# A fused attention and expert kernel: low halves of x written at once, all keys in one buffer, expert weights started a chunk earlier

## The chip, the cores and the metric

The kernel runs on one core of a Trainium2 chip. A core has a matrix engine (PE, whose weight loads are listed apart as PEld), a vector engine (DVE), a scalar engine (ACT), a GpSimd engine (POOL) and a queue engine (SP) that here only starts transfers. Each works through its own instructions in order, and they wait for one another through semaphores. The metric is device time in microseconds (us), the median of several runs.

## What is computed

Attention over 2 batches, 12 heads, 448 positions and head size 64, with a mix over heads ahead of the softmax and another behind it; then two expert layers on the 896 tokens.

```python
scores = scale * np.matmul(q, k.transpose(0, 1, 3, 2))
scores = np.einsum('bhij,hg->bgij', scores, w_pre)
attn = np.exp(scores - max); attn = attn / (sum + 1e-09)
attn = np.einsum('bhij,hg->bgij', attn, w_post)
x = np.matmul(attn, v)                 # -> [896, 768]
h = x @ w_in;  g = h * clip(h + 3, 0, 6) / 6;  x = g @ w_out
h = x @ w2_in; g = P(h) / Q(|h|);               out = g @ w2_out
```

Expert weights arrive as 64-bit numbers and are converted on the chip. Matrix products that must be exact are made of three: each operand is split into a high part (rounded to fp32r) and a low part (the rest), and high·high, high·low and low·high are added.

## The kernel before

**Attention.** Each batch has four chunks of query rows (12, 12, 12 and 9 groups of ten rows), eight chunks in all, numbered 0 to 7. The loop at L541 goes over chunks, the loop at L564 over the groups of a chunk. One pass of it is called a step here, and "step 6.11" is group 11 of chunk 6. There are 90 steps. The order of instructions on every engine is the order in which this code is written (a manual schedule).

In a step PE does, in this order: M, the head mix of this group's scores (`premix`, L277 to L279); A, the head mix of the weights of two groups ago (`postmix`, L312, eight entries); X, the product with the values (`av_unit`, L332, 16 matmuls) in some steps, for the chunk before; and scores of the next chunk (sc, L246) in some steps. DVE takes the maximum of M (L281), ACT the exponential e (L283). In the next step ACT copies A out (at, L316) and scales the mixing weights by the reciprocal sums (wr, L296). PE's A for a group waits for its wr. POOL splits the scores of the group two steps ahead into sh and sl (`gsplit`, L265, L267).

Two lists delay work: `preps` are run on ACT right behind the exponential of the next step, and their VectorE half (`lows`) a step later; `xposts` are run on ACT ahead of the next step's exponential and on DVE behind its maximum.

**Keys and x.** `XH` and `XL` hold the high and low part of x for the experts. While attention runs they lend their room: the keys of batch 0 (high and low) lie in XH, those of batch 1 in XL (L181). Batch 1's keys are loaded and split two at a time in chunks 0, 1 and 2 (L554). So x of the first 688 tokens goes to a separate `x1` when X leaves PSUM (L346 to L349), and is split into XH and XL later: `x_hi` copies 568 columns per row block in steps 6.0 to 6.5 (L614), `x_split` the remaining 120 columns and the whole low part, 688 columns, in steps 7.0 to 7.5 (L612). Later tokens are split straight out of PSUM (L351 to L356).

**Experts' first weights.** At the start of chunk 7 the pool `front` (queries, keys, staging) is released and the pool `late` is opened in its room (L559). Two weight units (768 KB each) are loaded from ACT's queue; the table `WST` says how many passes of their conversion (`split_pieces`, L406 to L422) run in each step: ACT scale, DVE shift, two DVE merges, then POOL split. The first expert product (h) starts in step 7.7.

**Values.** `load_v` loads values by pairs of heads into three buffers (`vraw`), each when the X that used the buffer is done. For chunk 7 these loads come at the end of attention, behind step 7.8, where six X units run one after another (L637).

Of the kernel before, what the change touches and what calls it, by code (L numbers as in the profile page):

```python
# [24 lines left out]
NCH = 4  # L25
# [24 lines left out]
def fused_kernel(  # L50
# [56 lines left out]
    x1 = x1p.tile([128, KD, XRAW], F32, name="x1")  # L107
# [17 lines left out]
    def load_v(C, hp):  # L125
        if C < len(chunks):
            t = att.tile([JP, 2, JC * D], F32, tag="vraw", bufs=3, name=f"vraw{C}_{hp}")
            nc.sync.dma_start(out=t, in_=v[chunks[C][0], hp])
            vraw[(C, hp)] = t

# [50 lines left out]
    ksts = [x.rearrange("p c t -> p (c t)").rearrange("p (x h s) -> p x h s", x=2, s=S) for x in (XH, XL)]  # L181
# [27 lines left out]
    def k_prep(b, hp):  # L209
        src = kraw[(b, hp // 2)][:, hp % 2, :]  # L210
        hi, lo = ksts[b][:, 0, hp, :], ksts[b][:, 1, hp, :]
# [21 lines left out]
    def scores(C, hp, tags=("sc", "sc"), st=None):  # L233
        n = chunks[C][3] * GR
        kh, kl = ksts[chunks[C][0]][:, 0, hp, :], ksts[chunks[C][0]][:, 1, hp, :]
# [104 lines left out]
    def av_evac(C, h, X):  # L340
# [5 lines left out]
        if t0 < XRAW:  # L346
            take = [lambda: None, lambda: None]
            take[h != 7] = lambda: (nc.vector.tensor_copy if h != 7 else nc.scalar.copy)(out=x1[:, cs, ts_], in_=src)
            xposts.append(take)  # L349
        else:  # L350
            xposts.append([  # L351
                lambda: nc.scalar.activation(out=XH[:, cs, ts_], in_=src, func=AF.Copy),
                lambda: nc.vector.tensor_tensor(
                    out=XL[:, cs, ts_], in0=src, in1=XH[:, cs, ts_].bitcast(F32), op=ALU.subtract
                ),
            ])  # L356
# [117 lines left out]
    def x_hi(c, a, b):  # L474
        nc.scalar.activation(out=XH[:, c, a:b], in_=x1[:, c, a:b], func=AF.Copy)

    def x_split(c):
        xposts.append([
            lambda: x_hi(c, XEAR, XRAW),
            lambda: nc.vector.tensor_tensor(  # L480
                out=XL[:, c, :XRAW], in0=x1[:, c, :], in1=XH[:, c, :XRAW].bitcast(F32), op=ALU.subtract
            ),
        ])
# [53 lines left out]
    WST = [0, 0, 1, 2, 1, 1, 2, 1, 1]  # L537
# [3 lines left out]
    for C, (b, r0, n, G) in enumerate(chunks):  # L541
# [11 lines left out]
        if C < 3:  # L553
            add([lambda: load_k(1, C), lambda: k_prep(1, 2 * C), lambda: k_prep(1, 2 * C + 1)], [8, 10, 11])  # L554
# [3 lines left out]
        if nxt is None:  # L558
            front.release()  # L559
            pools["late"] = tc.alloc_tile_pool(name="late", bufs=1, side="right", reuse_waits="tile")  # L560
            load_unit(units[0], nc.scalar)
# [318 lines left out]
```

## Time and profile before

| | |
|---|---|
| median of 3 runs | 763.8 us (762.0 to 770.0) |
| profiled execution | 766.65 us, span 764.9 us |
| PE busy | 722.0 us (94%) |
| DVE, ACT, POOL busy | 540.3, 426.4, 256.7 us |
| mean granted PE clock | 0.984 |
| PE, idle in all for ACT's wr | 14.9 us |

The span is the time from the first to the last instruction of the profiled execution; the run's own time is 1.75 us longer. PE is busy for most of the span, so what matters is where PE is not busy or slow, and what it waits for there.

### The profile page before, as it was taken

The numbers are of one execution on the slowest core, as the hardware profiler recorded it, in microseconds if no ns is written. First come the engines' busy times: TensorE is split into PE (matmuls) and PEld (weight loads), VectorE is DVE, ScalarE is ACT, GpSimd is POOL, SyncE is SP. The second block draws the span as 40 slices with busy tenths as digits, with TensorE's granted clock in tenths as the row PEclk, the third lists the DMA queues.
The fourth block names the chain that finished last, engine by engine and source line by source line (L and its number), as shares of the span: only waits on it lengthen the run. The fifth ranks groups of instructions, "written<-read, shape, count | busy, mean of one in ns | idle before, by whom it ended". The sixth has DMA issues, their size and how long they took to land.

```text
span 764.9 us, 12178 instructions
## 1 busy us (share of the span) xinstructions
PE 722.0 (94%) x4457; PEld 620.7 (81%) x4457; DVE 540.3 (71%) x947; ACT 426.4 (56%) x862; POOL 256.7 (34%) x255
## 2 busy tenths in 40 slices
PE   5899999999997889999999999999999998999996
PEld 2567777777776879888888888889899887999986
DVE  5564655545447749767655555569999999999996
ACT  4586666667676534443431111247667566689872
POOL 1776665666667525444344444300000000000000
PEclk8899999999999999999999999999999999999999
DMA  6545445445334435343333333334433353401002
GB/s 188 179 133 166 123 130 183 138 136 149 111 115 142 133 100 155 112 124 97 98 110 106 103 97 100 122 109 137 124 124 124 124 165 125 134 31 63 1 1 83
DMA packets 63283, 89.76 MB, mean 117 GB/s; under 512 B 5172, under 2 KB 53880, under 8 KB 63224
## 3 DMA queue, kind: packets, MB, share of 16 engines
q1 hardware_dynamic: 61024, 86.98, 36.7%
q10 hardware_dynamic: 2136, 2.01, 0.9%
q8 instruction: 35, 0.57, 0.3%
q14 instruction: 24, 0.20, 0.1%
q0 software_dynamic: 64, 0.01, 0.1%
HBM read 66.87 MB, written 2.75 MB: 91 GB/s over the span
## 4 chain that ended last, share of the span: by engine, by line
PE 70%; DVE 17%; ACT 6%; DMA 4%; issue 2%; SPq 0%; ACTq 0%; DVEq 0%
PE h L362 8%; PE h L364 8%; PE h L363 8%; PE A L312 8%; PE X L332 5%; PE y L364 5%; PE y L363 5%; PE y L362 5%; PE sc L246 5%; PE M L277 4%; PE M L279 2%; PE M L278 2%; DVE st L281 2%; PE acc L363 2%; PE acc L364 2%
## 5 line engine op out<-in xcount | busy, mean ns | idle before, releaser
L362 PE MATMUL h<-xh,wh 128*128 128x512 f32 (+1 forms) x384 | 143.2, 373 | 2.9 <-DVE u L714 1.7
L364 PE MATMUL h<-xh,wl 128*128 128x512 f32 (+1 forms) x384 | 141.4, 369 | 2.1 <-DVE wl L425 2.1
L363 PE MATMUL h<-xl,wh 128*128 128x512 f32 (+1 forms) x384 | 141.8, 369 | 0.0
L406 ACT ACTIVATE wf<-wraw 128x768 f32<-128x768 f32 (+1 forms) x50 | 43.8, 876 | 124.0 <-POOL wl L422 102.8
L312 PEld LDWEIGHTS A<-wr,e 120*112 120x112 f32 x720 | 82.4, 177 | 32.6 <-ACT wr L296 29.3
L312 PE MATMUL A<-wr,e 120*112 120x120 f32 x720 | 92.2, 271 | 15.2 <-ACT wr L296 14.9
L267 POOL TENSOR_TENSOR sl<-full,sh 120x448 fp32r<-120x448 f32 x89 | 103.3, 1161 | 7.4
L281 DVE TENSOR_REDUCE st<-M 120x1 f32<-120x448 f32 x90 | 56.1, 623 | 70.1 <-PE M L279 65.7
L283 ACT ACTIVATE e<-M,st 120x448 f32<-120x448 f32 x90 | 57.1, 635 | 73.8 <-DVE st L281 73.6
L362 PEld LDWEIGHTS h<-xh,wh 128*128 128x128 f32 x384 | 72.8, 190 | 12.9 <-DVE u L714 2.8
L364 PEld LDWEIGHTS h<-xh,wl 128*128 128x128 f32 x384 | 73.0, 190 | 12.1 <-DVE wl L425 3.3
L265 POOL TENSOR_SCALAR sh<-full 120x448 fp32r<-120x448 f32 x89 | 53.1, 597 | 85.4 <-PE M L278 54.5
L408 DVE TENSOR_SCALAR wf<-wf 128x768 int32<-128x768 int32 (+1 forms) x50 | 27.4, 549 | 76.7 <-ACT wf L406 76.7
L363 PEld LDWEIGHTS h<-xl,wh 128*128 128x128 f32 x384 | 72.9, 190 | 8.0
L421 POOL TENSOR_SCALAR wh<-wf 128x768 fp32r<-128x768 f32 (+1 forms) x34 | 33.1, 975 | 137.5 <-PE h L363 57.1
L364 PE MATMUL y<-gh,wl 128*128 128x384 f32 x192 | 70.8, 368 | 0.0
L363 PE MATMUL y<-gl,wh 128*128 128x384 f32 x192 | 70.2, 366 | 0.0
L362 PE MATMUL y<-gh,wh 128*128 128x384 f32 x192 | 69.9, 364 | 0.0
L422 POOL TENSOR_TENSOR wl<-wf,wh 128x768 fp32r<-128x768 f32 (+1 forms) x34 | 65.8, 1934 | 2.8
L316 ACT ACTIVATE at<-A 112x480 f32<-112x480 f32 x90 | 51.6, 574 | 5.4 <-PE A L312 5.3
L414 DVE SCALAR_TENSOR_TENSOR wf<-wraw,icst,wf 128x768 int32<-128x768 int32 (+1 forms) x50 | 51.2, 1026 | 0.8
L410 DVE SCALAR_TENSOR_TENSOR wf<-wraw,icst,wf 128x768 int32<-128x768 int32 (+1 forms) x50 | 50.3, 1007 | 0.9
(118 smaller groups left out, 1523.3 us busy)
## 6 DMA issues: line engine op xcount, KB each, us to landing
wraw<-in_moe_w_in_dram SPq DMA_DIRECT2D x30, 768.0 KB
wraw<-in_moe_w_out_dram SPq DMA_DIRECT2D x28, 768.0 KB
full<-stg SPq DMA_DIRECT2D x60, 210.0 KB
vraw<-in_v_dram SPq DMA_DIRECT2D x48, 224.0 KB
full<-stg SPq DMA_DIRECT2D x24, 157.5 KB
wraw<-in_moe_w_out_dram SPq DMA_DIRECT2D x6, 512.0 KB
kraw<-in_k_dram SPq DMA_DIRECT2D x6, 448.0 KB
qraw<-in_q_dram SPq DMA_DIRECT2D x6, 360.0 KB
```

Of the source, the lines that this page charges most:

```text
L265: eng.tensor_scalar(out=sh[:r], in0=s[:r], scalar1=1.0, scalar2=0.0, op0=ALU.mult, op1=ALU.add)
L267: return eng.tensor_tensor(out=sl[:r], in0=s[:r], in1=sh[:r].bitcast(F32), op=ALU.subtract)
L281: nc.vector.tensor_reduce(out=st[:r, 0:1], in_=mt[:r, :S], op=ALU.max, axis=AX.X, negate=True)
L283: nc.scalar.activation(out=e[:r], in_=mt[:r, :S], func=AF.Exp, bias=st[:r, 0:1], accum_out=st[:r, 1:2])
L312: nc.tensor.matmul(av[:, jc], lhsT=e[:r, jc * JP : (jc + 1) * JP], rhs=wr[:r, :, :rr], start=True, stop=True)
L316: lambda: nc.scalar.activation(out=at[C][:, :, :, c0 : c0 + rr], in_=av, func=AF.Copy)
L362: nc.tensor.matmul(o, lhsT=wh, rhs=mh, start=first, stop=False)
L363: nc.tensor.matmul(o, lhsT=wh, rhs=ml, start=False, stop=False)
L364: nc.tensor.matmul(o, lhsT=wl, rhs=mh, start=False, stop=last)
L410: nc.vector.scalar_tensor_tensor(out=wi, in0=hw, scalar=icst[:, 0:1], in1=wi, op0=ALU.bitwise_and, op1=ALU.bitwise_or)
L414: nc.vector.scalar_tensor_tensor(out=wi, in0=lw, scalar=icst[:, 1:2], in1=wi, op0=ALU.logical_shift_right, op1=ALU.bitwise_or)
L422: nc.gpsimd.tensor_tensor(out=lv, in0=w, in1=hv.bitcast(F32), op=ALU.subtract)
```

## The change

Both batches' keys now share XH, so XL is free from the start. Batch 1's keys are loaded in steps 2.4 to 2.6 and split in steps 2.9 to 3.1 (ACT), after the last scores of batch 0. Every X is split as it leaves PSUM: ACT writes the high part to x1 (now of the rounded type) or XH, DVE writes the low part to XL. `x_split` and `x_hi` go; `x_move` copies the high parts from x1 to XH on ACT (568 columns, six times, in steps 6.10 to 7.3, and 6 x 120 columns in step 7.4). The pool `late` is opened at the end of step 6.8; its first two units are loaded from SP's queue; one conversion pass runs in every step from 6.11 on. The values of chunk 7 are loaded in step 7.1 by six transfers into a buffer of the tag `full`.

```diff
@@ -104,7 +104,7 @@
     XH = xp.tile([128, KD, NT], F32R, name="xh")
     XL = xp.tile([128, KD, NT], F32R, name="xl")
     XRAW = S + 2 * CH
-    x1 = x1p.tile([128, KD, XRAW], F32, name="x1")
+    x1 = x1p.tile([128, KD, XRAW], F32R, name="x1")
 
 
     qraw = {}
@@ -123,10 +123,18 @@
         kraw[(b, m)] = t
 
     def load_v(C, hp):
-        if C < len(chunks):
+        if C < len(chunks) - 1:
             t = att.tile([JP, 2, JC * D], F32, tag="vraw", bufs=3, name=f"vraw{C}_{hp}")
             nc.sync.dma_start(out=t, in_=v[chunks[C][0], hp])
             vraw[(C, hp)] = t
+
+    def load_vs():
+
+        C = len(chunks) - 1
+        t = att.tile([JP, NP, 2, JC * D], F32, tag="full", bufs=2, name="vlast")
+        for hp in range(NP):
+            nc.sync.dma_start(out=t[:, hp], in_=v[chunks[C][0], hp])
+            vraw[(C, hp)] = t[:, hp]
 
 
     BF16 = mybir.dt.bfloat16
@@ -178,7 +186,7 @@
 
 
 
-    ksts = [x.rearrange("p c t -> p (c t)").rearrange("p (x h s) -> p x h s", x=2, s=S) for x in (XH, XL)]
+    kst = XH.rearrange("p c t -> p (c t)").rearrange("p (x h s) -> p x h s", x=2, s=S)
     qr = front.tile([128, NP, CH], F32R, name="qr")
     ql = front.tile([128, NP, CH], F32R, name="ql")
 
@@ -208,7 +216,7 @@
 
     def k_prep(b, hp):
         src = kraw[(b, hp // 2)][:, hp % 2, :]
-        hi, lo = ksts[b][:, 0, hp, :], ksts[b][:, 1, hp, :]
+        hi, lo = kst[:, 0, hp, :], kst[:, 1, hp, :]
         preps.append([
             lambda: nc.scalar.activation(out=hi, in_=src, func=AF.Copy),
             lambda: nc.vector.tensor_tensor(out=lo, in0=src, in1=hi.bitcast(F32), op=ALU.subtract),
@@ -232,7 +240,7 @@
 
     def scores(C, hp, tags=("sc", "sc"), st=None):
         n = chunks[C][3] * GR
-        kh, kl = ksts[chunks[C][0]][:, 0, hp, :], ksts[chunks[C][0]][:, 1, hp, :]
+        kh, kl = kst[:, 0, hp, :], kst[:, 1, hp, :]
         if hp == 0:
             full[C] = att.tile([GP, MG, S], F32, tag="full", bufs=2, name=f"full{C}")
         room(2)
@@ -343,17 +351,11 @@
         t0 = b * S + r0
         src = X[:, :, :n]
         cs, ts_ = slice(c0, c0 + 2), slice(t0, t0 + n)
-        if t0 < XRAW:
-            take = [lambda: None, lambda: None]
-            take[h != 7] = lambda: (nc.vector.tensor_copy if h != 7 else nc.scalar.copy)(out=x1[:, cs, ts_], in_=src)
-            xposts.append(take)
-        else:
-            xposts.append([
-                lambda: nc.scalar.activation(out=XH[:, cs, ts_], in_=src, func=AF.Copy),
-                lambda: nc.vector.tensor_tensor(
-                    out=XL[:, cs, ts_], in0=src, in1=XH[:, cs, ts_].bitcast(F32), op=ALU.subtract
-                ),
-            ])
+        o = (x1 if t0 < XRAW else XH)[:, cs, ts_]
+        xposts.append([
+            lambda: nc.scalar.activation(out=o, in_=src, func=AF.Copy),
+            lambda: nc.vector.tensor_tensor(out=XL[:, cs, ts_], in0=src, in1=o.bitcast(F32), op=ALU.subtract),
+        ])
 
 
     pools = {}
@@ -471,16 +473,8 @@
     build_mix()
     XEAR = S + CH
 
-    def x_hi(c, a, b):
-        nc.scalar.activation(out=XH[:, c, a:b], in_=x1[:, c, a:b], func=AF.Copy)
-
-    def x_split(c):
-        xposts.append([
-            lambda: x_hi(c, XEAR, XRAW),
-            lambda: nc.vector.tensor_tensor(
-                out=XL[:, c, :XRAW], in0=x1[:, c, :], in1=XH[:, c, :XRAW].bitcast(F32), op=ALU.subtract
-            ),
-        ])
+    def x_move(cs, a, b):
+        preps.append([lambda: nc.scalar.copy(out=XH[:, cs, a:b], in_=x1[:, cs, a:b].bitcast(F32)), lambda: None])
 
     first = gsplit(0, nc.vector)
     gsplit(1)
@@ -534,7 +528,7 @@
     SST = {12: [0, 1, 3, 4, 6, 7], 9: [0, 1, 2, 3, 4, 5]}
     QST = {12: [8, 9], 9: [6, 7]}
     AVST = {12: [2, 5, 8, 9, 11, 11], 9: [2, 3, 5, 6, 8, 8]}
-    WST = [0, 0, 1, 2, 1, 1, 2, 1, 1]
+    PRE, LATE = B * NCH - 2, 9
     manual = tc.manual_schedule()
     manual.__enter__()
     m = 0
@@ -550,17 +544,14 @@
             add([lambda h=h: scores(nxt, h) for h in range(NP)], SST[G])
         if C + 2 < len(chunks):
             add([lambda: q_prep(C + 2, 0, NP // 2), lambda: q_prep(C + 2, NP // 2, NP)], QST[G])
-        if C < 3:
-            add([lambda: load_k(1, C), lambda: k_prep(1, 2 * C), lambda: k_prep(1, 2 * C + 1)], [8, 10, 11])
+        if C == NCH - 2:
+            add([lambda m=m: load_k(1, m) for m in range(3)], [4, 5, 6])
+            add([lambda h=h: k_prep(1, h) for h in range(NP - 1)], [8, 8, 9, 10, 11])
+        if C == NCH - 1:
+            add([lambda: k_prep(1, NP - 1)], [0])
         if C > 0:
             add([lambda h=h: av_unit(C - 1, h) for h in range(1, H, 2)], [("av", a) for a in AVST[G]])
 
-        if nxt is None:
-            front.release()
-            pools["late"] = tc.alloc_tile_pool(name="late", bufs=1, side="right", reuse_waits="tile")
-            load_unit(units[0], nc.scalar)
-            load_unit(units[1], nc.scalar)
-            ucur[0] = 2
         for s in range(G):
             if s == 0 and C + 2 < len(chunks):
                 load_q(C + 2)
@@ -588,30 +579,35 @@
             xposts.clear()
             posts.clear()
             banks_of.clear()
-            if nxt is None:
-                for _ in range(WST[s]):
-                    next(wpieces)
+            if C > PRE or (C == PRE and s == G - 1):
+                next(wpieces)
             if m >= LAG:
                 postmix(m - LAG)
             for u in sched.get(("av", s), []):
                 u()
             for u in sched.get(s, []):
                 u()
-            if nxt is None and s == 0:
+            if C == PRE and s == LATE - 1:
+                flush()
+                front.release()
+                pools["late"] = tc.alloc_tile_pool(name="late", bufs=1, side="right", reuse_waits="tile")
+                load_units(1)
                 wpieces = (p for u in units[:4] for p in split_pieces(u))
-            if nxt is None and s == 4:
+            if C == PRE and s >= LATE:
+                x_move(s - LATE, 0, XEAR)
+            if C > PRE and s < KD - 3:
+                x_move(s + 3, 0, XEAR)
+            if C > PRE and s == 3:
+                x_move(slice(0, KD), XEAR, XRAW)
+            if C > PRE and s == 1:
+                load_vs()
+            if C > PRE and s == 4:
                 load_units(2)
-            if nxt is None and s == 7:
-                load_units(3)
             if nxt is None and s >= 7:
                 if s == 7:
                     h100 = gemm1(0, 0, ps.tile([128, 512], F32, tag="sc", bufs=3, name="h1_0_0"))
                 for _ in range(3):
                     next(h100)
-            if nxt is None and s < KD:
-                x_split(s)
-            if nxt == len(chunks) - 1 and s < KD:
-                x_hi(s, 0, XEAR)
             m += 1
 
     C = len(chunks) - 1
@@ -633,7 +629,8 @@
     for _ in range(2):
         next(h110)
     drain()
-    pieces(3)
+    load_units(3)
+    pieces(2)
     for h in range(1, H, 2):
         av_unit(C, h)
         flush()
```

Where rows move. On ACT, in steps 6.11 to 7.1 (e is the exponential, at and wr belong to the two groups before, x is x1, xh is XH, wf is a weight unit); before:

```order
L283 ACTIVATE e_3000,st_2998<-M_2994,st_2998 120x448
L389 DMA wraw<-in_moe_w_in_dram 128x6x256 x2
L316 ACTIVATE at_2705<-A_3004 112x48x10
L296 ACTIVATE wr_3039<-wq,st_2976 120x120
L283 ACTIVATE e_3051,st_3049<-M_3045,st_3049 120x448
L316 ACTIVATE at_2705<-A_3056 112x48x10
L296 ACTIVATE wr_3062<-wq,st_2998 120x120
L475 ACTIVATE xh<-x_86 128x120
L283 ACTIVATE e_3075,st_3073<-M_3069,st_3073 120x448
```

and after the change:

```order
L291 ACTIVATE e_3020,st_3018<-M_3014,st_3018 120x448
L477 CAST xh<-x_86 128x568
L408 ACTIVATE wf<-wraw 128x768
L324 ACTIVATE at_2718<-A_3027 112x48x10
L304 ACTIVATE wr_3054<-wq,st_2994 120x120
L356 ACTIVATE x_86<-X_9_3032 128x2x120
L291 ACTIVATE e_3067,st_3065<-M_3061,st_3065 120x448
L477 CAST xh<-x_86 128x568
L324 ACTIVATE at_2718<-A_3074 112x48x10
L304 ACTIVATE wr_3080<-wq,st_3018 120x120
```

The two transfers have left this queue, and copies of x and a scaling pass stand between an exponential and the at and wr behind it.

On DVE, from the maximum of step 7.3 on; before:

```order
L281 TENSOR_REDUCE st_3135<-M_3131 120x1
L291 TENSOR_SCALAR st_3097<-st_3097 120x1
L292 RECIPROCAL st_3097<-st_3097 120x1
L480 TENSOR_TENSOR xl<-x_86,xh 128x688
L408 TENSOR_SCALAR wf<-wf 128x768
L410 SCALAR_TENSOR_TENSOR wf<-wraw,icst,wf 128x768
L281 TENSOR_REDUCE st_3172<-M_3168 120x1
L291 TENSOR_SCALAR st_3135<-st_3135 120x1
L292 RECIPROCAL st_3135<-st_3135 120x1
L353 TENSOR_TENSOR xl<-X_1_3112,xh 128x2x120
L480 TENSOR_TENSOR xl<-x_86,xh 128x688
L414 SCALAR_TENSOR_TENSOR wf<-wraw,icst,wf 128x768
```

and after the change:

```order
L289 TENSOR_REDUCE st_3157<-M_3153 120x1
L299 TENSOR_SCALAR st_3121<-st_3121 120x1
L300 RECIPROCAL st_3121<-st_3121 120x1
L289 TENSOR_REDUCE st_3197<-M_3193 120x1
L299 TENSOR_SCALAR st_3157<-st_3157 120x1
L300 RECIPROCAL st_3157<-st_3157 120x1
L357 TENSOR_TENSOR xl<-X_1_3135,xh 128x2x120
L410 TENSOR_SCALAR wf<-wf 128x768
L289 TENSOR_REDUCE st_3224<-M_3220 120x1
L299 TENSOR_SCALAR st_3197<-st_3197 120x1
L300 RECIPROCAL st_3197<-st_3197 120x1
L412 SCALAR_TENSOR_TENSOR wf<-wraw,icst,wf 128x768
```

The low parts of x of 688 columns are gone, and one weight pass at most stands between two maxima.

On SP's queue, from chunk 6's end on (vraw are values of chunks 6 and, second time round, 7; wraw weight units); before:

```order
L128 DMA vraw_5_2930<-in_v_dram 112x512
L128 DMA vraw_0_2962<-in_v_dram 112x512
L128 DMA vraw_1_3018<-in_v_dram 112x512
L128 DMA vraw_2_3028<-in_v_dram 112x512
L128 DMA vraw_3_3121<-in_v_dram 112x512
L128 DMA vraw_4_3157<-in_v_dram 112x512
L389 DMA wraw<-in_moe_w_in_dram 128x6x256
L128 DMA vraw_5_3227<-in_v_dram 112x512
L128 DMA vraw_0_3263<-in_v_dram 112x512
L389 DMA wraw<-in_moe_w_in_dram 128x6x256
L128 DMA vraw_1_3331<-in_v_dram 112x512
L128 DMA vraw_2_3341<-in_v_dram 112x512
```

and after the change:

```order
L128 DMA vraw_5_2940<-in_v_dram 112x512
L391 DMA wraw<-in_moe_w_in_dram 128x6x256 x2
L128 DMA vraw_0_2980<-in_v_dram 112x512
L128 DMA vraw_1_3041<-in_v_dram 112x512
L128 DMA vraw_2_3051<-in_v_dram 112x512
L136 DMA vlast<-in_v_dram 112x512 x6
L128 DMA vraw_3_3144<-in_v_dram 112x512
L128 DMA vraw_4_3183<-in_v_dram 112x512
L391 DMA wraw<-in_moe_w_in_dram 128x6x256
L128 DMA vraw_5_3245<-in_v_dram 112x512
L391 DMA wraw<-in_moe_w_in_dram 128x6x256 x13
```

Two weight units now stand ahead of chunk 6's values, and chunk 7's values ahead of the second half of those of chunk 6.

## Rows read from the trace of the kernel before

**Rows 1.** Waits of PE: engine, line, releaser, us in total, times, longest.
```profile
PE A L312 <- ACT wr L296: 14.9, 22, 2.0
PE X L332 <- DMA vraw<-in_v_dram: 2.8, 2, 1.5
```
**Rows 2.** Timeline of PE, steps 6.10 to 7.0: start, length, instruction [idle before].
```profile
227.38 1.04 PE L332 MATMUL X<-at,vraw 112*64 112x120 f32 x16
228.35 0.47 PE L277 MATMUL M<-sh,wp_h 120*120 120x448 f32 x1
...
229.07 0.98 PE L312 MATMUL A<-wr,e 120*112 120x120 f32 x8
229.81 0.44 PE L277 MATMUL M<-sh,wp_h 120*120 120x448 f32 x1
...
231.45 1.07 PE L312 MATMUL A<-wr,e 120*112 120x120 f32 x8 [0.78 <-ACT wr L296]
...
234.24 0.46 PE L277 MATMUL M<-sh,wp_h 120*120 120x448 f32 x1
```
**Rows 3.** Timeline of ACT in step 6.10.
```profile
229.93 0.64 ACT L283 ACTIVATE e<-M,st 120x448 f32<-120x448 f32 x1 [0.88 <-DVE st L281]
```
**Rows 4.** Timeline of PE, steps 7.5 to 7.8.
```profile
245.62 0.44 PE L277 MATMUL M<-sh,wp_h 120*120 120x448 f32 x1
...
248.39 1.07 PE L312 MATMUL A<-wr,e 120*112 120x120 f32 x8 [1.92 <-ACT wr L296]
...
250.37 0.46 PE L277 MATMUL M<-sh,wp_h 120*120 120x448 f32 x1
...
256.13 0.73 PE L277 MATMUL M<-sh,wp_h 120*120 120x448 f32 x1
...
259.86 0.36 PE L277 MATMUL M<-sh,wp_h 120*120 120x448 f32 x1
```
**Rows 5.** Timeline of DVE in the same stretch.
```profile
247.32 1.23 DVE L480 TENSOR_TENSOR xl<-x,xh 128x688 fp32r<-128x688 f32 x1
248.47 1.89 DVE L414 SCALAR_TENSOR_TENSOR wf<-wraw,icst,wf 128x768 int32<-128x768 int32 x1
250.28 0.61 DVE L281 TENSOR_REDUCE st<-M 120x1 f32<-120x448 f32 x1
```
**Rows 6.** The chain of work that ended last, three places: start, us, what.
```profile
204.05 0.57 ACT xh L475
...
251.65 0.79 ACT wf L406
...
268.26 2.00 PE X L332 x48
270.27 4.30 DMA vraw<-in_v_dram
274.62 1.44 PE X L332 x16
276.06 0.62 PE h L362
```
**Rows 7.** Stretches: us, PE, PEld, DVE, ACT, POOL busy, PE clock, DMA share, GB/s.
```profile
170.50:193.00 22.50, 22.50 (x186) 17.65 (x184) 11.94 (x35) 15.37 (x41) 15.42 (x19) 1.00 0.52 151
201.80:225.80 24.00, 23.23 (x186) 17.05 (x184) 11.97 (x35) 18.66 (x47) 15.34 (x18) 1.00 0.36 108
276.00:278.50 2.50, 2.50 (x11) 2.50 (x10) 0.90 (x2) 2.40 (x5) 0.00 (x0) 0.61 0.01 2
```
**Rows 8.** Groups by line and shape: count | busy us, mean ns | idle before.
```profile
L213 ACT ACTIVATE xl<-kraw 128x448 fp32r<-128x448 f32 x6 | 3.4, 568 | 0.0
L214 DVE TENSOR_TENSOR xl<-kraw,xl 128x448 fp32r<-128x448 f32 x6 | 6.4, 1072 | 0.0
L214 DVE TENSOR_TENSOR xh<-kraw,xh 128x448 fp32r<-128x448 f32 x6 | 3.6, 621 | 0.8 <-ACT xh L213 0.8
L352 ACT ACTIVATE xh<-X 128x240 fp32r<-128x240 f32 x3 | 1.1, 376 | 0.9 <-PE X L332 0.9
L353 DVE TENSOR_TENSOR xl<-X,xh 128x240 fp32r<-128x240 f32 x3 | 1.2, 395 | 1.5 <-ACT xh L352 1.5
```

## The prediction

> **What bounds the kernel now.** I read the page first: PE is busy for 94% of the span, so a gain must come from places where PE stands still or runs slowly. The waits of PE name two causes that the change touches: A waiting for wr, 14.9 us in 22 places, and X waiting for the values, 2.8 us in two [rows 1]. The timeline then shows where. In the chain of waits the second cause is the end of attention: 48 X matmuls take 2.00 us, then 4.30 us pass on a transfer of values, then 16 more take 1.44 us, and the h matmuls behind them run slowly [rows 6]; from 276.0 to 278.5 the granted clock is 0.61, between its levels of 1.2 and 2.4 GHz [rows 7].
>
> The first cause follows a rule that one quiet stretch gives. A step with only M and A takes 229.81 − 228.35 = 1.46 us, an X adds 228.35 − 227.38 = 0.97 [rows 2]. M of step 6.10 starts at 228.35, its exponential at 229.93, and the A that needs its wr at 231.45, 3.1 us after M [rows 2, 3]. Step 6.11 has two X and takes 4.43 us; 1.46 + 2 × 0.97 = 3.40, so 1.03 of it is the stall (0.78 idle and a slower restart) [rows 2]. The bare step ahead of it hid 1.46 of the loop, hence the loop needs 1.46 + 1.03 = 2.49 us of cover. I use: stall of a step = 2.49 + P − length of the step before, not below 0, where P is what ACT does between the exponential of the step before and its at and wr. A step with X and scores covers 2.49; a bare one does not. Whatever delays a maximum on DVE adds like P: in step 7.5 DVE spends 1.23 us on a low part of x and 1.89 on a weight pass, so that the maximum of an M that started at 245.62 runs only at 250.28 [rows 4, 5]. Steps 7.5 and 7.6 take 4.75 and 5.76 us, and M of step 7.7 shows the low clock, 0.73 us where others take 0.46 [rows 2, 4].
>
> **The change part by part.**
>
> *Values at once.* From the first X to the h matmuls before: 276.06 − 268.26 = 7.80 us. With the values there, 96 matmuls at the pace of the first 48 take 4.00 [rows 6]: −3.8. They are loaded in step 7.1 and needed after step 7.8, over 20 us later, against 4.3 for a late one. The clock need not fall either: 2.5 us at 0.61 is 1.5 us of work at full clock [rows 7]: −1.0. Both bounds: 0 if something else holds X, −4.8 if nothing does; I take −4.8, since the products ahead of X are the same and the copies of A that X needs were in time.
>
> *Copies of x out of chunk 6.* Six ACT copies of 0.57 [rows 6] stood in steps 6.0 to 6.5 between exponential and wr. Steps 5.0 to 5.8 take 22.5 us, steps 6.0 to 6.8, with the same 186 matmuls, 24.0 [rows 7]. The copies move to 6.10 to 7.3, where I count them below: −1.5 here.
>
> *Chunk 7.* DVE loses six low parts (1.23 us in the row shown) and has one weight pass a step, 1.89 in that row, beside a maximum of 0.61 [rows 5], in steps that come out at 2.4 and more; it may be late by a few tenths, and I add nothing. ACT gets more between exponential and wr: P is 0.57 in 6.10, 0.57 + 0.79 (the scaling pass, [rows 6]) in 6.11, 0.57 in 7.0 to 7.2, 1.36 again in 7.3, about 0.72 in 7.4 (720 columns at the rate of 568), 0.79 in 7.7. A stall of more than 1.03 also pushes the next exponential back by the excess, since wr stands ahead of it; in 7.4, where X is copied out as well (0.28 of it beyond its neighbours), by 1.39 − 1.03 + 0.28 = 0.64. Then by the rule: 6.11: stall 2.49 + 0.57 − 1.46 = 1.60, step 4.99; 7.0: 1.45 (4.99 covers all); 7.1: stall 1.61, 3.06; 7.2: 2.49 + 0.57 + 0.6 − 3.06 = 0.60, with X 3.02; 7.3: 2.46; 7.4: 2.49 + 1.36 − 2.46 = 1.39, 2.84; 7.5: 2.49 + 0.72 + 0.64 − 2.84 = 1.01, 3.43; 7.6: 2.42; 7.7: 1.46 + 1.5 for nine h matmuls + 0.07 = 3.03; 7.8 gets 0.25 more. The sum from 6.11 to 7.7 is 26.7; before it was 259.86 − 229.81 = 30.05 [rows 2, 4]. So −3.35 + 0.25 = −3.1. Bounds: with all P at 0 the same steps give 23.6, −6.4; with DVE's passes at 1.9 and each exposed, nothing is left, 0. I take −3.1, because ACT's durations hardly vary and DVE has room. POOL splits the first unit in step 7.3 now, ahead of the split of scores for 7.6; it has three steps for both, 8.7 us by this sum, and each us beyond them would cost one.
>
> *Keys.* Six ACT passes of 0.57 (0.47 where they overlap their neighbours, as the others do) and six DVE low parts leave the ends of chunks 0 to 2 and crowd into 2.9 to 3.1. Of the four passes that leave chunks 0 and 1, two were followed by a step that could not cover them: −0.94. Of the new ones, two together in 2.9 lengthen the bare step 2.10 by 0.94; DVE's backlog of two low parts there ends in the long step 2.11; those in 3.0 and 3.1 expose some 0.36. Net +0.4. The low part now goes to XH, where the row shows 0.62, but that row is the start of the kernel; beside POOL the row shows 1.07 [rows 8], which I take. Bounds for the whole: −0.9 with none of the new ones exposed, +1.9 with all six.
>
> *Split out of PSUM.* Eighteen evacuations of chunks 0 to 5 change: ACT's 0.38 instead of a DVE copy in twelve, DVE's 0.40 instead of ACT's copy alone in six [rows 8]. ACT starts it when X ends, just ahead of M, and the exponential waits 1.6 us after M's start for the maximum: hidden, 0. Without that cover it would be 12 × 0.28 = 3.3. DVE's six fall ahead of the long step 11.
>
> *Queues.* ACT no longer issues two transfers; that was in the long step 6.11, so 0. On SP the two units wait for the last staging to be read, and the values of 7.2 stand behind them. Two units are 1.57 MB; at the 151 GB/s that chunk 5 averages [rows 7] that is 10.4 us, and from M of 6.8 to X of 7.2 are over 16. The first unit alone would take 5.2 us, and its scaling pass in 6.11 comes some 10 us after M of 6.8. I charge 0; three us late would cost about 2, since 7.0 is bare but 6.11 leaves 1.1 of cover.
>
> **Sum.** −4.8 − 1.5 − 3.1 + 0.4 = −9.0 us. The profiled execution took 766.65, so 757.6; it lay 2.9 above the median of the runs shown, so against 763.8 the forecast is about 755.
>
> **Rivals.** *The stalls of chunk 7 are only exchanged* (copies of x and scaling passes on ACT for low parts on DVE). For it: 6.3 us of stall remain in my own sum from 6.11 to 7.7, and POOL slows DVE's passes up to 1.89. Against: ACT's rows hardly vary. Then −9.0 + 3.1 = −5.9: 758.
>
> *The wait for values moves forward.* vraw 3 to 5 of chunk 6 stand behind six transfers of chunk 7, and steps 7.6 and 7.8 need them. For it: one such wait cost 4.3. Against: three steps lie between the load of vraw 5 and its use, over 8 us. Then the 3.8 come back: 759.
>
> *Slower: the clock.* Before, the clock fell after stalls of 1.92 and 2.0 and after the wait for values [rows 1, 4, 7]. Mine has four stalls of 1.0 to 1.6 between 6.11 and 7.5. If they bring the clock down and keep it there, each us of PE work at 1.2 GHz costs one more. From 6.11 to the end of X, PE has 26.7 − 6.3 + 8.4 + 4.0 = 33 us of work (8.4 is step 7.8 up to X, 268.26 − 259.86). Half of it at the low level is +16.5, about 771.5; below 9 us of such work the kernel still gains. Against: the bare ends of chunks have stalls of 1.0 every time, with the clock at 1.00 [rows 2, 7]. The Trainium skill, "TensorE: Matmul & The Clock Gate", Part 1, says that the slow clock is the default state and that activity releases it; by that the shorter stalls are on the safe side of those that brought the clock down, but no row here shows where the limit is.
>
> *The scaling pass comes before its data* (first unit late by 3 us): +2, 757; counted into the first case.
>
> **How the numbers follow.** Forecast (753 to 757.5): 0.58. Stalls exchanged, 758: 0.27. Wait moved, 759: 0.09. Clock, slower: 0.06. The ends of the bounds are −13.6 (4.8 + 1.5 + 6.4 + 0.9: 750) and −1.1 (4.8 + 1.5 − 1.9 − 3.3: 762.7). For eight in ten I take 750.5 to 761.5. A measurement of this kernel tells about 1%, 7.6 us, from no change, so the border is 756.2, close above the forecast: the forecast's case is on the faster side nine times in ten, and the second case seldom: faster 0.55, within 1% 0.39, slower 0.06.
>
> **What would show it.** Right: no X waiting for values at the end, 96 X in about 4 us, clock 1.00 behind them; steps 6.0 to 6.8 in 22.5 us; 6.11 to 7.7 in about 27 with waits for wr of 1.0 to 1.6 us in 6.11, 7.1, 7.4 and 7.5; a long 2.10. Wrong: ACT's wf waiting for a transfer in 6.11, X of 7.6 or 7.8 waiting for values, an exponential behind an x copy in steps 6 and 0 of earlier chunks, or expert products later that wait for weights and so give the gain back (they are paced by PE now).

## The result, and the profile after

| | before | after |
|---|---|---|
| median of 12 runs each | 765.84 us (762.0 to 770.0) | 758.55 us (757.32 to 760.78) |
| ratio to before, 95% interval | | 0.9902 (0.9885 to 0.9919) |
| profiled execution, span | 766.65, 764.9 us | 760.78, 759.1 us |
| PE, idle in all for ACT's wr | 14.9 us, 22 times | 14.8 us, 21 times |

The change takes 7.3 us off, about 1% (by the interval 6.2 to 8.8); the forecast was 9.0. The measured 758.55 is inside the stated range of 750.5 to 761.5, but outside the 753 to 757.5 of the forecast's own case and next to the 758 of its first rival. It lies 3.7 us above 763.8 − 9.0 = 754.8. Of these, 2.0 are the base, since the median of before is 765.84 with twelve runs and was 763.8 with three, and 1.7 are the change. Which case it was can't be read from the median, but from the stages below.

The page after: the head and PE's row of part 1, and the chain of waits at the end of attention (start, us, what).

```profile
span 759.1 us, 12175 instructions
PE 719.2 (95%) x4457; PEld 620.4 (82%) x4457; DVE 537.3 (71%) x947; ACT 429.6 (57%) x869; POOL 256.1 (34%) x255
```
```profile
268.27 0.17 PE h L366
268.44 3.79 PE X L340 x96
```

These are the lines that answer [rows 6]: 96 X without a stop in 3.79 us, where 48 X, 4.30 us of transfer and 16 X stood. The chain leaves out 32 X of before, which ran while it followed the last transfer. PE's timeline before shows them, and that PE itself stood for 1.54 and 1.22 us:

```profile
271.77 1.63 PE L332 MATMUL X<-at,vraw 112*64 112x88 f32 x32 [1.54 <-DMA vraw<-in_v_dram]
274.62 1.44 PE L332 MATMUL X<-at,vraw 112*64 112x88 f32 x16 [1.22 <-DMA vraw<-in_v_dram]
```

The waits of PE after (engine, line, releaser, us in total, times, longest) name no wait for values any more. The wait for wr, of [rows 1], comes out at the same total, but not because it only moved:

```profile
PE A L320 <- ACT wr L304: 14.8, 21, 1.4
```

Summed from PE's timelines, A waited for wr for 0.77 us in chunk 6 up to step 6.10 and for 5.82 in steps 6.11 to 7.7 before; after, it is none and 4.61. What makes up for this in the first profile after is 1.1 us more in chunks 1 to 3, where the keys now stand, and 0.7 in chunks 0, 4 and 5. The second profile of the changed kernel has 13.5 in all.

Stretches of the profile after (us, then busy time of PE, PEld, DVE, ACT, POOL, granted PE clock, DMA share, GB/s): chunk 5's steps 0 to 8 by its old bounds, steps 6.0 to 6.8, and the 2.5 us behind the last X.

```profile
170.50:193.00 22.50, 22.08 (x196) 17.64 (x196) 11.48 (x35) 15.65 (x44) 16.04 (x19) 1.00 0.44 131
202.00:224.40 22.40, 22.40 (x197) 17.34 (x196) 10.84 (x32) 15.11 (x42) 15.52 (x19) 1.00 0.34 100
272.20:274.70 2.50, 2.50 (x15) 2.36 (x14) 0.92 (x3) 2.42 (x5) 0.00 (x0) 1.00 0.00 0
```

Against [rows 7]: chunk 6 now runs at the pace of chunk 5, and the clock behind X is 1.00, not 0.61. The timeline of PE in steps 6.11 to 7.6 shows where the waits for wr have gone (start, length, instruction, idle before):

```profile
233.25 1.07 PE L320 MATMUL A<-wr,e 120*112 120x120 f32 x8 [1.35 <-ACT wr L304]
...
239.72 1.07 PE L320 MATMUL A<-wr,e 120*112 120x120 f32 x8 [1.35 <-ACT wr L304]
...
241.74 1.07 PE L320 MATMUL A<-wr,e 120*112 120x120 f32 x8 [0.33 <-ACT wr L304]
...
248.15 1.07 PE L320 MATMUL A<-wr,e 120*112 120x120 f32 x8 [0.97 <-ACT wr L304]
...
250.46 1.92 PE L320 MATMUL A<-wr,e 120*112 120x120 f32 x8 [0.61 <-ACT wr L304]
252.31 1.81 PE L340 MATMUL X<-at,vraw 112*64 112x120 f32 x16
```

They stand in the steps of the forecast: 6.11, 7.1, 7.2, 7.4 and 7.5. In the last A and the X behind it the work itself is slow, 1.92 and 1.81 us where 1.07 and 1.04 are usual: the clock fell. In the stretch from 250.4 to 254.0 the granted clock is 0.53, the lower of its levels for nearly all of it.

```profile
250.40:254.00 3.60, 3.54 (x24) 3.12 (x24) 1.41 (x4) 1.59 (x5) 3.00 (x3) 0.53 0.16 53
```

### The profile page after: what moved, and what is told of

Read it like the earlier page. It is cut to its first block, busy times and chain, and to the rows that moved or that the text cites. A ratio compares the mean times of both kernels' runs of the same rounds, so it can differ in the third digit from the quotient of the medians.

```text
span 759.1 us, 12175 instructions
## 1 busy us (share of the span) xinstructions
PE 719.2 (95%) x4457; PEld 620.4 (82%) x4457; DVE 537.3 (71%) x947; ACT 429.6 (57%) x869; POOL 256.1 (34%) x255
## 4 chain that ended last, share of the span: by engine, by line
PE 72%; DVE 16%; ACT 5%; DMA 4%; issue 2%; SPq 0%; ACTq 0%; DVEq 0%
PE h L366 9%; PE h L364 8%; PE A L320 8%; PE h L365 8%; PE y L364 5%; PE X L340 5%; PE y L365 5%; PE y L366 5%; PE sc L254 5%; PE M L285 4%; PE M L287 2%; PE M L286 2%; PE acc L365 2%; PE acc L366 2%; DVE u L713 2%
## 5 line engine op out<-in xcount | busy, mean ns | idle before, releaser
L320 PE MATMUL A<-wr,e 120*112 120x120 f32 x720 | 92.7, 272 | 14.8 <-ACT wr L304 14.8
```

The source lines that it names most:

```text
L320: nc.tensor.matmul(av[:, jc], lhsT=e[:r, jc * JP : (jc + 1) * JP], rhs=wr[:r, :, :rr], start=True, stop=True)
```

## Where the time went, stage by stage

Differences between starts of instructions in the timelines of PE (M of a step to M of the next, X, h and so on). "Again" and "third" are two more profiles of the changed kernel, told of below.

| us | before | after | again | third |
|---|---|---|---|---|
| chunks 1 to 3 | 90.57 | 91.61 | 90.98 | 90.96 |
| steps 6.0 to 6.8 | 24.00 | 22.40 | 22.40 | 22.41 |
| steps 6.11 to 7.7 | 30.05 | 28.74 | 27.12 | 27.13 |
| step 7.8 up to the last X run | 8.33 | 8.58 | 8.60 | 8.58 |
| that X run up to h | 7.80 | 3.79 | 3.79 | 3.79 |
| first h product up to the first y | 114.29 | 113.41 | 113.41 | 113.41 |
| chunk 0 | 27.80 | 29.14 | 28.62 | 29.26 |
| chunks 4 and 5 | 61.82 | 62.11 | 61.54 | 61.71 |
| third product (acc) to the end | 238.14 | 237.64 | 236.33 | 237.76 |
| span | 764.9 | 759.1 | 753.9 | 757.0 |

The first six rows are those that the prediction spoke of. They sum to −6.5 us in the first profile (+1.04 − 1.6 − 1.31 + 0.25 − 4.01 − 0.88) and to −8.8 us in the two others; the forecast was −9.0. For the next three rows the prediction counts nothing. They differ between executions of the very same code, chunk 0 by 0.6 us among the three of the changed kernel, acc to the end by 1.4. That chunk 0 was shorter in the one profile of before is no effect of the change either: with the values alone, whose chunk 0 is that of before, it took 29.54, and the steps 0.8 to 0.11, which lost two keys' passes, are the same to 0.01 us.

## The experiments

**The changed kernel again.** Twice, unaltered. The first of the two was to show whether chunk 0, 29.1 us in the first profile after, goes back to the 27.8 of before (chance) or stays (the change). It took 28.62, neither of the two; the spread named above answers it better. Recorded for the second:

> The changed kernel once more, unaltered, for one question: whether the low clock after the stalls of steps 6.11 to 7.5 comes in every execution or only in some. In its first profile the clock fell in step 7.5, which then took 5.06 us, in its second it stayed at 1.00 and the step took 3.45. Theory (chance): either of the two values, with 6.11 to 7.4 the same to 0.1 us in both cases (5.00, 1.46, 3.04, 3.16, 2.59, 2.69). Rival (the first profile was a different course of the same steps): 6.11 to 7.4 differ, and the clock goes with that difference.

The first gave 757.69 us (755.64 to 759.17), ratio 0.9905 (0.987 to 0.994); the second is a single run of 758.7 us. In both, steps 6.11 to 7.4 are as in the first profile (5.00, 1.45, 3.03 to 3.04, 3.16, 2.59, 2.70), with the same stalls ahead of A. The timeline of PE of "again":

```profile
230.99 1.07 PE L320 MATMUL A<-wr,e 120*112 120x120 f32 x8 [1.35 <-ACT wr L304]
...
237.44 1.07 PE L320 MATMUL A<-wr,e 120*112 120x120 f32 x8 [1.35 <-ACT wr L304]
...
239.46 1.07 PE L320 MATMUL A<-wr,e 120*112 120x120 f32 x8 [0.33 <-ACT wr L304]
...
245.88 1.07 PE L320 MATMUL A<-wr,e 120*112 120x120 f32 x8 [0.98 <-ACT wr L304]
...
248.20 1.07 PE L320 MATMUL A<-wr,e 120*112 120x120 f32 x8 [0.62 <-ACT wr L304]
```

But here the last A takes 1.07 us and the step 3.45, and the granted clock of that place is 1.00:

```profile
248.10:251.00 2.90, 2.80 (x29) 2.46 (x30) 1.43 (x4) 1.63 (x5) 2.82 (x3) 1.00 0.17 59
```

So the low clock in step 7.5, worth 1.6 us, comes in some executions and not in others after the same stalls: it fell in one of three profiles of this kernel. Two kernels below do the same work in steps 6.11 to 7.5 (late values, keys not split), and there step 7.5 took 3.46 and 3.44, so it is one in five.

**The values alone.** The kernel before with one part of the change.

```diff
-        if C < len(chunks):
+        if C < len(chunks) - 1:
...
+    def load_vs():
+        C = len(chunks) - 1
+        t = att.tile([JP, NP, 2, JC * D], F32, tag="full", bufs=2, name="vlast")
...
+            if nxt is None and s == 1:
+                load_vs()
```

> The kernel before, with one part of the change alone: the values of chunk 7 loaded at once in step 7.1. Theory: the wait at the end of attention goes, 96 X in 3.8 to 4.0 us instead of 7.8, and the low clock behind them: -4.8 us against before (ratio 0.9937). Rival, the loads collide with those of chunk 6's values or weights and the wait comes back in steps 7.6 to 7.8: 0 to -1.

760.6 us (759.36 to 763.95) against the 764.31 of before on the same chip, ratio 0.9945 (0.9923 to 0.9967), by which the load takes 4.2 us off. Its chain of waits has the one X run in place of the wait, and its window right behind the first h shows the clock at 1.00:

```profile
271.81 3.79 PE X L340 x96
```
```profile
275.90:278.40 2.50, 2.50 (x15) 2.27 (x14) 1.27 (x3) 2.50 (x6) 0.00 (x0) 1.00 0.00 0
```

The stages of this kernel are 3.79 and 113.41 us as after the change, and 23.99 and 30.11 (steps 6.0 to 6.8, 6.11 to 7.7) as before it. By the ratios over half of the gain is this one load (0.55% of 0.98%).

**The values late again.** The changed kernel with the old loads for chunk 7.

```diff
-        if C < len(chunks) - 1:
+        if C < len(chunks):
...
-            if C > PRE and s == 1:
-                load_vs()
```

> The changed kernel with that one part undone: values of chunk 7 in three rotating buffers again. Theory: the wait and the low clock behind it are back, +4.8 us against the changed kernel, so about 763.3 (ratio to before 0.996 to 0.997). Rival, the gain of the change came from elsewhere: about 758.5.

762.32 us (759.75 to 765.17), ratio 0.9959 (0.9933 to 0.9985), 3.8 to 4.6 slower than the two medians of the changed kernel. The chain of waits has the transfer back:

```profile
265.61 2.00 PE X L340 x48
267.62 3.84 DMA vraw<-in_v_dram
271.51 0.83 PE X L340 x16
```

From the first X to h it is 6.73 us, 2.9 more than 3.79, not 4.0 more: the transfer took 3.84 where it took 4.30, the last 16 X took 0.83 at full clock where they took 1.44 in [rows 6], and the clock stayed up behind them (113.42 from h to y). PE's timeline shows that the second of its two waits was shorter, 0.77 us against 1.22, the first as long (1.56 and 1.54):

```profile
271.51 0.83 PE L340 MATMUL X<-at,vraw 112*64 112x88 f32 x16 [0.77 <-DMA vraw<-in_v_dram]
```

Whether the clock stayed up because of that or by chance, these two profiles do not show.

**The copies of x on GpSimd.**

```diff
-        preps.append([lambda: nc.scalar.copy(out=XH[:, cs, a:b], in_=x1[:, cs, a:b].bitcast(F32)), lambda: None])
+        preps.append([lambda: nc.gpsimd.tensor_scalar(out=XH[:, cs, a:b], in0=x1[:, cs, a:b].bitcast(F32),
+            scalar1=1.0, scalar2=0.0, op0=ALU.mult, op1=ALU.add), lambda: None])
```

> The changed kernel with the seven copies of x from x1 to XH on GpSimd instead of ACT, so that nothing of them stands between an exponential and the at and wr behind it. Theory (stall = 2.49 + P - step): 6.11 falls from 5.0 to 4.4, 7.1 from 3.0 to 2.5, 7.2 to 2.5, 7.4 to 2.3, 7.5 to 2.7, and the low clock of 7.5 goes if it followed from these stalls: -5 us against the changed kernel, about 753.5 (ratio to before 0.984). Rival, GpSimd's split of the scores comes late instead and M waits for it: no gain or a loss, with M's wait for sl in chunk 7. Rival, the low clock is chance and stays: -3.4.

758.76 us (755.91 to 761.6), ratio 0.9926 (0.9897 to 0.9955): no better than the change itself, and 5 us above the theory. The first rival is what happened; steps 6.11 to 7.7 take 28.81 us. Steps 6.11 and 7.1 fell from 5.00 and 3.04 to 4.44 and 2.47 as the rule says with P at 0; step 7.2 kept its 3.16. But step 7.5 took 4.39 (3.45), since M stood waiting for POOL, which had a copy and the passes of a weight unit ahead of the split of scores. PE, then POOL:

```profile
250.58 0.46 PE L285 MATMUL M<-sh,wp_h 120*120 120x448 f32 x1 [1.16 <-POOL sh L273]
251.81 0.52 PE L287 MATMUL M<-sl,wp_h 120*120 120x448 f32 x1 [0.56 <-POOL sl L275]
```
```profile
245.62 0.67 POOL L477 TENSOR_SCALAR xh<-x 128x568 fp32r<-128x568 f32 x1
246.25 1.13 POOL L423 TENSOR_SCALAR wh<-wf 128x768 fp32r<-128x768 f32 x1
247.47 1.82 POOL L424 TENSOR_TENSOR wl<-wf,wh 128x768 fp32r<-128x768 f32 x1
249.26 1.27 POOL L273 TENSOR_SCALAR sh<-full 120x448 fp32r<-120x448 f32 x1
```

Behind this the clock fell too (0.88 from 248.0 to 262.0, step 7.6 at 5.02). A stall was taken from one engine and given to another.

**Each copy of x on ACT twice.** One run.

```diff
-        preps.append([lambda: nc.scalar.copy(...), lambda: None])
+        for _ in range(2):
+            preps.append([lambda: nc.scalar.copy(...), lambda: None])
```

> The changed kernel with each ACT copy of x from x1 to XH made twice. Theory (stall = 2.49 + P - step, and a stall over 1.03 pushes the next exponential): 6.11 5.6 us (was 5.0), 7.1 3.6 (was 3.0), 7.2 3.6, 7.3 2.6, 7.4 3.3 (was 2.7), 7.5 4.2 (was 3.45), sum of 6.11 to 7.7 29.8 (was 27.1), without a low clock; one low stretch would add up to 1.7. Rival, the copies lie in idle time of ACT: 27.1 again.

767.51 us, span 765.8, against a median of 766.74 of before on the same chip: in this one run the whole gain is gone. Steps 6.11 to 7.7 take 33.89 us (27.1), 4.1 more than the 29.8 of the theory, and A waits longer where the rule says so. Another 1.8 to 3.2 us are in the stretch from acc to the end, 239.51 us, which the copies do not touch. Its timeline of PE, steps 6.11, 7.1 and 7.4:

```profile
233.63 1.07 PE L320 MATMUL A<-wr,e 120*112 120x120 f32 x8 [2.04 <-ACT wr L304]
...
242.38 1.07 PE L320 MATMUL A<-wr,e 120*112 120x120 f32 x8 [2.04 <-ACT wr L304]
...
252.13 1.94 PE L320 MATMUL A<-wr,e 120*112 120x120 f32 x8 [1.66 <-ACT wr L304]
```

P grew by one copy, some 0.6 us, each of these stalls by 0.69 (1.35, 1.35 and 0.97 with single copies). So ACT's work between an exponential and its wr does set these stalls. What the theory missed is the clock: it fell twice behind them, in 6.11 (granted clock 0.80 over the step, which took 7.07 us where 5.6 was expected) and in 7.4 to 7.5 (0.79 and 0.51). This is the prediction's slower rival at work, with stalls of 1.66 to 2.04 us, which the change does not have; and even here the clock came back within two steps.

**The old table of weight passes.** One run.

```diff
+    WST = [0, 0, 1, 2, 1, 1, 2, 1, 1]
...
-            if C > PRE or (C == PRE and s == G - 1):
-                next(wpieces)
+            if C > PRE:
+                for _ in range(WST[s]):
+                    next(wpieces)
...
-    pieces(2)
+    pieces(3)
```

> The changed kernel with the weight passes at the old steps (none in 6.11, 0, 0, 1, 2, 1, 1, 2, 1, 1 in 7.0 to 7.8), all else as changed. Theory: ACT's scaling pass goes from 6.11 and 7.3 to 7.2 and 7.5, DVE's double steps delay a maximum by under 1 us: steps 6.11 to 7.7 take 26 to 28 us, as with one pass a step (27.1 without a low clock). Rival, one pass a step is what ended the stalls of 7.5 and 7.6: they come back, 29 us or more.

758.38 us. Steps 6.11 to 7.7 take 27.39 us against 27.12: 7.3 and 7.5 are longer (3.26 and 4.30 for 2.59 and 3.45), 7.4 is shorter (1.46 for 2.70). But step 7.8 up to the last X run takes 8.33, as before the change, against 8.60, so up to X both come to 35.72: one pass a step is worth nothing in all. With the same table steps 7.5 to 7.7 took 4.75, 5.76 and 3.73 before, and 4.30, 2.60 and 3.13 here, without the 688-column low parts on DVE. So by exclusion it is their going, not the table, that ended the long stalls there; no run takes out the low parts alone.

**Batch 1's keys not split.** One run.

```diff
+        if b == 1:
+            return
         preps.append([
```

> The changed kernel without the split of batch 1's keys (six ACT passes, six DVE low parts in steps 2.9 to 3.2 are left out, the loads stay; batch 1 is computed with batch 0's keys). It gives the price of the keys where they stand now. Theory: step 2.10 falls from 2.66 to about 1.72, and 3.0 to 3.2 together to about 8.2 (2.42 + 2.48 + 3.40 - a little): -1.3 to -1.8 us in chunks 2 and 3. Rival, the passes are hidden: 2.10 stays at 2.4 or more.

755.17 us, span 753.5. Step 2.10 takes 1.73 us (2.66 with the keys), chunks 1 to 3 take 89.59 (90.96). In their new place the keys cost 1.4 us; in their old place, by the same sum, 90.57 − 89.59 = 1.0. The move costs 0.4.

**The copies put elsewhere.** Four of the six long copies on GpSimd, in the steps where the trace shows it idle, two on ACT in long steps, the last one on ACT in step 7.8.

```diff
+    MOVES = {(PRE, 9): [(0, True)], (PRE, 10): [(1, True), (2, True), (3, False)], (PRE + 1, 1): [(4, False), (5, True)]}
...
-            if C == PRE and s >= LATE:
-                x_move(s - LATE, 0, XEAR)
-            if C > PRE and s < KD - 3:
-                x_move(s + 3, 0, XEAR)
-            if C > PRE and s == 3:
+            for c, pool in MOVES.get((C, s), []):
+                x_move(c, 0, XEAR, pool)
+            if C > PRE and s == 7:
```

> The changed kernel with the seven copies placed by the rule: GpSimd takes one in 6.10, two in 6.11, one in 7.2; ACT takes one in 6.11 and one in 7.2, where the steps cover them, and the 6 x 120 columns in 7.8. Theory: 6.11 4.4, 7.1 2.5, 7.4 2.1, 7.5 2.9, sum of 6.11 to 7.7 24.8 us against 27.1, no wait of M for GpSimd, and with the stalls smaller fewer low clocks: -2.3 to -4 against the changed kernel, 754.5 to 756 (ratio to before 0.985 to 0.988). Rival, GpSimd is late again and M waits as in the version with all copies there: 758 or more.

756.01 us (754.03 to 758.15), ratio 0.9876 (0.9845 to 0.9907). Steps 6.11 to 7.7 take 25.29 us (27.12), and the waits of PE for wr have shrunk:

```profile
PE A L320 <- ACT wr L304: 11.5, 19, 1.2
```

In 6.11 and 7.1 what is left, 0.78 each, is the stall of a bare end without any work in the way, the one of [rows 2]. No M waits for GpSimd. Single steps miss the theory by more than in the change: 7.4 took 1.79 (2.1), 7.5 3.27 (2.9), and the sum is 0.5 above the 24.8 forecast. By the runs alone the gain over the change is not clear, since the two intervals overlap; the stage shows it, here and in the next kernel (25.31).

**The keys put elsewhere as well.** On top of the last.

```diff
-            add([lambda h=h: k_prep(1, h) for h in range(NP - 1)], [8, 8, 9, 10, 11])
+            add([lambda h=h: k_prep(1, h) for h in range(3)], [10, 10, 10])
...
-            add([lambda: k_prep(1, NP - 1)], [0])
+            add([lambda h=h: k_prep(1, h) for h in range(3, NP)], [1, 1, 2])
```

> The kernel with the copies of x put elsewhere (the run before this one: 756.0, span 752.5) with the passes of batch 1's keys put elsewhere as well: three in step 2.11, two in 3.2, one in 3.3, where the step is long enough to cover them by the rule (4.43 against 2.49 + 1.71; 3.55 against 2.49 + 1.14; 3.39 against 2.49 + 0.57). Theory (the keys cost 1.4 us, in step 2.10 and in chunk 3, because of where their ACT passes stand): 2.10 back at 1.73 (there 2.66), chunk 3 at about 26.5 (there 27.05), chunks 2 and 3 together 1.4 shorter, 754.6. Rival (the passes cost their place on DVE, wherever they are put): three low parts in 2.11 hold the maximum of 3.0 or the scores of 3.0, 3.0 grows by 1 us or more, nothing gained, 756.

754.7 us (753.34 to 756.13), ratio 0.9853 (0.9832 to 0.9874), the fastest of all. But not by the keys: step 2.10 is back at 1.73 as the theory said, and 3.0 grew from 2.42 to 3.49 as the rival said, so that chunks 2 and 3 take 59.01 us against 59.15. The median forecast, 754.6, was met by luck. DVE, then PE, at step 3.0:

```profile
114.57 0.62 DVE L289 TENSOR_REDUCE st<-M 120x1 f32<-120x448 f32 x1 [3.01 <-PE M L287]
...
115.67 2.08 DVE L222 TENSOR_TENSOR xh<-kraw,xh 128x448 fp32r<-128x448 f32 x3
```
```profile
116.74 0.47 PE L254 MATMUL sc<-xh,qr 64*120 64x448 f32 x2 [0.80 <-DVE xh L222]
```

The low parts stand on DVE behind the maximum of 3.0; DVE was idle for 3.01 us just before, but in the order as written they come after it, and the first scores of 3.0 wait for them. The rule on ACT alone chose the place, and DVE's half of the same passes undid it. The two medians were taken on different chips; their ratios to before, 0.9853 and 0.9876, have intervals that overlap, and no stage shows a difference.

## Why the prediction was right, point by point

**Values at once: right.** −4.8 forecast; 4.01 from X to h and 0.88 of clock behind it (all of it in the first 2 us of h) are −4.9 in the trace, −4.2 by the ratio of the values alone. The clock part may not always be there to gain: with the late values put back it did not fall. No row says how often it does.

**Copies out of chunk 6: right.** −1.5 forecast, −1.6 in all three profiles.

**Chunk 7: the mechanism right, the size somewhat off, and a chance on top.** The rule on the cover of 2.49 us gave, for steps 6.11 to 7.7, and "again" measured:

| us | 6.11 | 7.0 | 7.1 | 7.2 | 7.3 | 7.4 | 7.5 | 7.6 | 7.7 | sum |
|---|---|---|---|---|---|---|---|---|---|---|
| forecast | 4.99 | 1.45 | 3.06 | 3.02 | 2.46 | 2.84 | 3.43 | 2.42 | 3.03 | 26.7 |
| measured | 5.00 | 1.45 | 3.03 | 3.16 | 2.59 | 2.70 | 3.45 | 2.59 | 3.14 | 27.1 |

The misses are small, 0.17 us at most: an X step without a stall takes 2.59, not 2.42 to 2.46 as I took for 7.3 and 7.6, and 7.2 has another limit. ACT's timeline before shows it: at of 7.2 waits until A of 7.1 has ended, and A of 7.2 follows it by at and wr.

```profile
238.44 0.59 ACT L316 ACTIVATE at<-A 112x480 f32<-112x480 f32 x1 [0.36 <-PE A L312]
```

A to A is 241.74 − 239.72 = 2.02 us there after the change, and the step took 3.16 before it and with the copies on GpSimd alike, so less P does not shorten it. So −2.7 with 7.8's 0.25, where −3.1 was forecast. In the first profile it is −1.1: there the clock fell in 7.5 (5.06). That was my slower rival's mechanism, and I gave it only as a clock that stays down; as a single short fall, with a chance and 1.6 us, it belonged into the forecast. The prediction put stalls shorter than 1.92 us on the safe side; in one profile of five they were not. The gain itself holds a clock term that my sum did not name. Of the 9.49 us of steps 7.6 and 7.7 before, some 1.5 are the low clock (granted 0.82 in both): at full clock they would take about 2.59 + 1.99 + 0.25 and 3.14, an estimate from the X step, the stall with its restart, and 7.7 after. With the values alone, where these steps have the code of before, the clock fell in them again (0.88 and 0.74). So of the −2.9 in steps 6.11 to 7.7 about 1.2 is A waiting less for wr (5.82 to 4.63 in "again") and about 1.5 a fall of the clock that did not come, and in the first profile it came all the same, one step earlier. The chain of waits after, from the copy of x behind the exponential of step 7.3 to the copy behind that of 7.4, which the wr for the A of 7.5 follows, shows how ACT is the path there, copy by copy (start, us, what):

```profile
246.00 0.56 ACT xh L477
246.56 0.80 ACT wf L408
247.36 0.46 ACT at L324
247.82 0.28 ACT wr L304
248.10 0.25 ACT xh L356
248.35 0.62 ACT e L291 x2
248.97 0.32 ACT xh L477
```

**Keys: the sum right by luck, its parts not.** +0.4 forecast and measured in two profiles, +1.0 in the first. The long 2.10 came as forecast (2.67; measured 2.65 and 2.66, and in "again" 2.37 with 0.28 more in 2.9). The gain at the old places was 0.56, not 0.94: 2.1 gave 0.48, and 1.0 only 0.08 (3.07 to 2.99). Step 1.0 too would have A following A by at and wr; that this is its limit I argue from 7.2, no run here shows it for it. Behind 2.10 the new places cost next to nothing (2.11 0.12 shorter, 3.2 0.15 longer in "third"), where 0.36 was forecast, and the two misses cancel. In the first profile the pair of low parts beside POOL took 2.46 us on DVE, in the third 1.51. It stood ahead of the maximum of 2.11, whose weights the A of 3.0 waits for, and 3.0 took 3.17 us instead of 2.44. The slow pair is not enough for that: in "again" it took 2.47, but began 0.17 us behind M of 2.11 and not 0.79, and 3.0 took 2.56. In the other kernels with this code 3.0 took 2.41 or 2.42. DVE in the first profile and in the third:

```profile
111.16 2.46 DVE L222 TENSOR_TENSOR xh<-kraw,xh 128x448 fp32r<-128x448 f32 x2
```
```profile
111.48 1.51 DVE L222 TENSOR_TENSOR xh<-kraw,xh 128x448 fp32r<-128x448 f32 x2
```

**Split out of PSUM and queues: nothing, as forecast.** The passes have the durations taken for them (0.38 and 0.40), ACT's copy ends ahead of the exponential's start in nearly every step; it delays it in 7.4, as the prediction counted, and in 2.10, where two key passes stand ahead of it. Neither the scaling pass in 6.11 nor X in 7.6 and 7.8 waits for a transfer, and no M waits for POOL's split of the scores. Groups by line and shape (count, busy us, mean ns, idle before):

```profile
L357 DVE TENSOR_TENSOR xl<-X,x 128x240 fp32r<-128x240 f32 x15 | 5.8, 390 | 0.3 <-ACT x L356 0.3
L356 ACT ACTIVATE x<-X 128x240 fp32r<-128x240 f32 x15 | 5.5, 368 | 3.0 <-PE X L340 3.0
L477 ACT CAST xh<-x 128x568 fp32r<-128x568 f32 x6 | 3.9, 657 | 0.0
```

**Why the median moved by 7.3 and not 9.** The terms sum to −8.8 in two profiles of after and to −6.5 in one, and the median of the runs lies between. That the fall of the clock in 7.5 and the long 3.0 come in some executions and not in others is shown; how often they come in the timed runs is not, since those have no trace. One more limit: before was profiled once. Its falls of the clock in 7.6 and 7.7 came again with the values alone, the one behind X has no second profile. Its y products also ran at a slower pace throughout (132.52 us up to acc, against 131.90 in the profiles after and in that with the values alone), 0.6 us that no term names. So the last us or so between −7.3 and −8.8 stays open.

**Rivals.** The wait for values did not move forward (no X waits for vraw). The stalls of chunk 7 were not merely exchanged, though the median alone, −7.3 between the forecast's −9.0 and this rival's −5.9, would not tell: steps 6.11 to 7.7 went from 30.05 us to 28.74 in the first profile and to 27.1 in the two others, where this rival has no change. New stalls did take back a part, as the forecast counted: 6.11 to 7.4 took 17.93 us in "again", 15.81 before, and steps 7.5 to 7.7 took 9.19 against 14.24.

## What to carry to other kernels

A step loop that runs over three engines has a cover, read in one quiet stretch (here 2.49 us), and with it a move of work on one engine could be sized step by step to 0.2 us in the changed kernel and to 0.4 in the one with the copies put elsewhere, as long as the clock stayed up; but each half of a moved pass needs the same sum on its own engine, as the keys' low parts on DVE show. Put moved work into the steps that are long for another reason, and split it over the engines that are idle there: that took another 1.8 us off steps 6.11 to 7.7. And where stalls of a us or so stand close together, a fall of the clock belongs into the forecast as a term with a chance, since the same code shows it in one execution and not in the next.

## What the runs showed of the hardware

**The clock falls after the same stalls in one execution and not in the next.** Waits of 1.35, 1.35, 0.33, 0.97 and 0.61 us had a granted clock of 0.53 behind them in one profile (250.4 to 254.0) and 1.00 in two others, with the same waits to 0.02 us. What makes the difference no run here shows. With each copy made twice, of two stalls of 2.04 us the one in 6.11 had a fall behind it, the one in 7.1 had none.

**A subtraction of two SBUF operands on DVE takes 0.62 us alone and up to about twice that beside POOL.** The low part of a key, 128 x 448, took 0.61 to 0.63 us alone and 1.01 to 1.32 beside POOL's split of scores in the changed kernel. Two of them on DVE, with a low part of x out of PSUM between them, and POOL's instruction:

```profile
114.76 0.62 DVE L222 TENSOR_TENSOR xh<-kraw,xh 128x448 fp32r<-128x448 f32 x1
...
116.52 0.39 DVE L357 TENSOR_TENSOR xl<-X,x 128x240 fp32r<-128x240 f32 x1
116.82 1.01 DVE L222 TENSOR_TENSOR xh<-kraw,xh 128x448 fp32r<-128x448 f32 x1
```
```profile
116.22 1.14 POOL L275 TENSOR_TENSOR sl<-full,sh 120x448 fp32r<-120x448 f32 x1
```

POOL's instruction ends at 117.36; from there to DVE's end at 117.83 is 0.47, so DVE did most of its work, 0.62 us when alone, behind it. The Trainium skill, "SBUF — State Buffer", section "SBUF: two separate sides", says that the port pair which the two engines share is an exclusive lock, and that, between a DVE instruction with two SBUF inputs and a GpSimd instruction that reads SBUF, whichever comes second is blocked until the other has ended. The trace agrees to 0.15 us: if nothing had been done before POOL's end, 0.62 and not 0.47 would be left behind it. The subtraction out of PSUM with one SBUF operand keeps its 0.39 us beside POOL. So the low parts of the first 688 tokens are shorter when they are made as X leaves PSUM (6.8 us in all against 8.3 before) and steadier: 0.39 to 0.41 us for each of 240 columns, against 1.01 to 1.77 for each of 688 columns before.
